# Three edits to a fused attention and feed-forward kernel: the last stores inside the Else of an If that is never taken, an interleave behind a normalisation, and two transposes a step ahead

## The chip, the cores and the metric

One core of a Trainium2 chip. The metric is the time of one execution in microseconds (us), median of several runs. Single runs scatter by about 1.2 us, as much as the effects that are looked for. So most of the argument is read from traces, and the times are used as a check. Engines in the profile: PE is TensorE (matmuls), PEld its weight loads, DVE is VectorE, ACT is ScalarE, POOL is GpSimd, SP is SyncE. A trailing q (SPq, DVEq, PEldq) marks work of an engine's instruction queue itself: branches, semaphore waits, issues of transfers.

## The reference

Causal attention with a decay bias from `s`, followed by a feed-forward layer with exact GELU. Eight batches of 576 tokens and eight heads of 64 give 4608 rows of 512.

```python
def _attn_ref(q, k, v, s):                      # q, k, v: 8 x 8 x 576 x 64, s: 8 x 8 x 576
    scores = scale * np.matmul(q, k.transpose(0, 1, 3, 2))
    cum = np.cumsum(np.maximum(s, 0.0), axis=-1)
    bias = -(cum[:, :, :, None] - cum[:, :, None, :])
    scores = np.where(causal, -1e9, scores + np.minimum(bias, 0.0))
    # ... softmax over the last axis ...
    return np.matmul(attn, v)

def _moe_ref(x, w_in, w_out):                   # 4608 x 512, 512 x 2048, 2048 x 512
    h = x @ w_in
    g = 0.5 * h * (1.0 + erf(h * inv_sqrt2))
    return g @ w_out
```

## The kernel before

The kernel works in nine chunks of 512 rows. While PE runs the feed-forward layers of chunk c (`l1_item`, `l2_item`), the attention of batch c + 1 is woven in (`sc_item`: scores and exp; `av_item`: weighted values and normalisation). The queries and keys of a later batch are interleaved by VectorE (GpSimd for batch 2), written to DRAM as rows and read back by a transposing DMA. For batches 0 and 1 PE does the transposes itself (`tr_items`); there the tile `early_q` holds the q and k of pairs 0 and 1, `early_k` those of pairs 2 and 3.

This is the weaving of chunks 1 and later, with the place of the k interleave:

```python
            late = c < 3
            for p in range(1, NP):
                # ... cut: early q interleave and transposes where not late ...
                sc_item(nb, p)
                av_item(nb, p - 1)
                l2_item(c, p, 0, 12)
                if p == NP - 1:
                    # ... cut: transposes of the rows, loads ...
                    av_item(nb, p)
                    norm_rest(nb)
                    gelu_set()
                l2_item(c, p, 12)
                # ...
                if nb + 1 < B and p == 2 and late:
                    interleave(nb + 1, "q")
                    write_rows(nb + 1, 0, nc.sync)
                if nb + 1 < B and p == 1 + late:          # late: behind q, ahead of pair 3
                    interleave(nb + 1, "k")
                    write_rows(nb + 1, 1, nc.sync)
```

The end of the program. `l2_last` does the last 128 rows in two halves of the columns; all fast pools are closed; then a flag is loaded that says whether the input leaves the range for which the fast path is right. If so, a long general path recomputes everything. With this input it is never entered.

```python
            for sub in range(4):
                if c == NCH - 1 and sub == 3:
                    l2_last(c, sub)          # two halves: 32 matmuls, copy, store each
                    break
                l2_item(c, sub, av=sub % 2 == 0)
                # ... cut: parts of the range check ...
    fast.close()

    rv = nc.values_load(bad[0:1, 0:1], min_val=0, max_val=1)
    with tc.If(rv > 0):
        # ... the general path: about 120 lines, not executed ...
```

The prologue, before the first chunk:

```python
    tr_items(0, 1, (0,))
    weights_pe()
    tr_items(0, 1, (1,))
    # ...
    sc_item(0, 1, neg=True, units=(1,))
    sc_item(0, 2, neg=True, units=(0,))
    tr_items(0, 3, (0,))
    tr_items(0, 3, (1,))
    sc_item(0, 2, neg=True, units=(1,))
```

## Time and profile before

| | before |
|---|---|
| median of the runs known ahead of the prediction | 328.77 us (327.85 to 329.01) |
| span of the profiled execution | 328.2 us |
| PE busy | 315.0 us (96%) |
| from the end of the last matmul to the end of the span | 6.01 us |

The profiled execution is one run among others, and here it was a slow one: that run took 330.29 us by the clock that gives the medians. A time is about 2 us longer than the span of its trace.

Two views of the kernel before that the prediction uses but does not show. The first is the page's line of the chain that ended last, followed back from the last instruction, as shares of the span by engine.

```profile
PE 76%; DMA 15%; POOL 4%; ACT 2%; DVE 1%; issue 1%; DVEq 0%; POOLq 0%
```

PE's matmuls make the chain for three quarters. Of the 47.6 us of DMA (15%), 37.2 are at the start, between 10.21 and 50.68, where the loads of weights and of batch 1 set the pace; the other 10.4 are the load of batch 3's k rows, 81.11 to 91.51. The second is the timeline of the last microseconds: start, duration, engine, line and operation, and in brackets the idle time before it.

```profile
318.52 3.66 PE L565 MATMUL o_ps<-w_out_r,gT 128*64 128x256 bf16 x64
...
320.47 0.42 DVE L570 COPY o_sb<-o_ps 128x256 f32<-128x256 f32 x1 [1.05 <-PE o_ps L565]
320.93 2.08 SPq L571 DMA_DIRECT2D out_dram<-o_sb  x2
322.22 0.42 DVE L570 COPY o_sb<-o_ps 128x256 f32<-128x256 f32 x1 [1.32 <-PE o_ps L565]
```

The last matmul ends at 322.19, the last copy at 322.64, the last store is issued at 322.67. Everything from there to 328.19 is landing, branch and closing waits.

### The profile page before, as it was taken

To read this page: it belongs to the slowest core of one execution; us is meant where nothing else is said; L and a number is where in the kernel's file an instruction comes from. 1 tells how busy PE (TensorE), PEld (TensorE's weight loads), DVE (VectorE), ACT (ScalarE), POOL (GpSimd) and SP (SyncE) were. 2 spreads that over 40 slices of the span, in tenths; PEclk is the share of its full clock that TensorE was granted. 3 is DMA by queue.
4 is the path that set the end of the run, shared out by engine and by line. 5 is a ranking of instruction groups with operands and counts; after the bars stand their busy time and mean duration, and the time that the engine had idled before them with its cause. 6 is when DMAs were issued, how large, how long until landed. Compare 5 with 4: busy or idle time off the path is not lost.

```text
span 328.2 us, 8740 instructions
## 1 busy us (share of the span) xinstructions
PE 315.0 (96%) x3753; PEld 182.9 (56%) x3755; DVE 191.8 (58%) x376; ACT 204.9 (62%) x292; POOL 69.6 (21%) x104
## 2 busy tenths in 40 slices
PE   7899997999999999999999999999999999999992
PEld 3566555666645556546655665556555655455562
DVE  6777446995579256937494748655884672150021
ACT  4796747759566767677667767677759676105400
POOL 8754243503400361005301700130000000000000
PEclk9999999999999999999999999999999999999998
DMA  7999999945994499967999899587700100010012
GB/s 119 222 210 208 233 188 266 245 96 43 245 281 107 88 225 241 209 97 213 257 151 158 219 272 112 106 245 193 126 2 34 65 35 2 34 64 34 1 66 72
DMA packets 53837, 47.45 MB, mean 145 GB/s; under 512 B 31328, under 2 KB 43872, under 8 KB 53792
## 3 DMA queue, kind: packets, MB, share of 16 engines
q0 software_dynamic: 15936, 23.07, 38.2%
q1 hardware_dynamic: 37856, 23.75, 30.9%
q8 instruction: 31, 0.51, 0.6%
q14 instruction: 14, 0.11, 0.1%
HBM read 36.85 MB, written 16.52 MB: 163 GB/s over the span
## 4 chain that ended last, share of the span: by engine, by line
PE 76%; DMA 15%; POOL 4%; ACT 2%; DVE 1%; issue 1%; DVEq 0%; POOLq 0%
PE h_ps L522 34%; PE o_ps L544 30%; DMA early_k<-in_k_dram 7%; DMA w_out_r<-in_moe_w_out_dram 5%; PE sc_ps L387 4%; PE avd L425 3%; PE avn L425 3%; DMA w_in_r<-in_moe_w_in_dram 3%; PE o_ps L565 1%; POOL raw_v L204 1%; PE avr L425 1%; ACT P L403 1%; POOL early_q L117 1%; POOL early_k L117 1%; POOL early_q L105 0%
## 5 line engine op out<-in xcount | busy, mean ns | idle before, releaser
L544 PE MATMUL o_ps<-w_out_r,gT 128*64 128x512 bf16 x1120 | 129.3, 380 | 0.0
L522 PE MATMUL h_ps<-xT,w_in_r 128*64 128x512 bf16 x1152 | 126.2, 379 | 0.6 <-DVE xT L461 0.6
L522 PEld LDWEIGHTS <-w_in_r 128*64 128x64 bf16 x1152 | 68.5, 110 | 56.3 <-issue 1.1
L544 PEld LDWEIGHTS <-gT 128*64 128x64 bf16 x1120 | 61.0, 110 | 49.9
L529 ACT ACTIVATE gT<-h_ps 128x1024 bf16<-128x1024 f32 x54 | 54.3, 1023 | 53.2 <-PE h_ps L522 53.2
L403 ACT ACTIVATE P<-sc_ps 128x1024 bf16<-128x1024 f32 x64 | 62.0, 1021 | 26.6 <-PE sc_ps L387 24.7
L551 DVE COPY o_sb<-o_ps 128x512 f32<-128x512 f32 x33 | 22.7, 687 | 49.1 <-PE o_ps L544 49.1
L412 DVE TENSOR_TENSOR P<-P,tri_bf 128x512 bf16<-128x512 bf16 x58 | 24.6, 432 | 42.9 <-ACT P L403 42.5
L215 DVE TENSOR_REDUCE amx<-qkT 128x2 f32<-128x1152 bf16 x32 | 40.9, 1335 | 0.0
L204 POOL DMA_DIRECT2D raw_v<-in_v_dram x40 | 34.5, 887 | 9.7 <-DMA early_q<-in_q_dram 2.5
L461 DVE SCALAR_TENSOR_TENSOR xT<-avn,ln 128x256 bf16<-128x256 f32 (+3 forms) x66 | 22.4, 386 | 20.5 <-ACT ln L442 14.0
L232 DVE TENSOR_TENSOR vv<-raw_v,wb 128x512 bf16<-128x512 f32 (+3 forms) x44 | 25.2, 632 | 0.7 <-DMA raw_v<-in_v_dram 0.7
L222 DVE TENSOR_REDUCE amv<-raw_v 128x1 f32<-128x2048 f32 (+1 forms) x16 | 23.0, 1470 | 2.3 <-DMA raw_v<-in_v_dram 2.3
L442 ACT ACTIVATE ln<-ln 128x512 f32<-128x512 f32 (+1 forms) x40 | 23.5, 587 | 1.3
L532 ACT ACTIVATE gT<-h_ps 128x512 bf16<-128x512 f32 x36 | 19.6, 602 | 6.3 <-PE h_ps L522 6.3
L441 ACT ACTIVATE ln<-avd 128x256 f32<-128x256 f32 x58 | 19.2, 391 | 6.8 <-PE avd L425 6.7
L387 PE MATMUL sc_ps<-qkT 64*128 64x256 bf16 (+2 forms) x320 | 21.1, 250 | 1.6 <-DVE qkT L372 0.6
L387 PEld LDWEIGHTS <-qkT 64*128 64x128 bf16 x320 | 12.9, 94 | 15.7 <-issue 12.4
L425 PEld LDWEIGHTS <-wb 128*64 128x64 bf16 x384 | 17.1, 110 | 4.6 <-issue 1.1
L425 PEld LDWEIGHTS <-vv 128*64 128x64 bf16 x384 | 17.6, 110 | 2.8 <-issue 1.0
L425 PE MATMUL avd<-P,wb 128*64 128x256 bf16 x232 | 16.7, 263 | 0.2 <-DVE P L412 0.2
L425 PE MATMUL avn<-P,vv 128*64 128x256 bf16 x232 | 16.0, 260 | 0.6 <-DVE xT L461 0.5
(101 smaller groups left out, 156.2 us busy)
## 6 DMA issues: line engine op xcount, KB each, us to landing
out_dram<-o_sb SPq DMA_DIRECT2D x35, 256.0 KB, 3.3
raw_v<-in_v_dram POOLq DMA_DIRECT2D x32, 256.0 KB, 8.8
rows<-qk_bf SPq DMA_DIRECT2D x12, 576.0 KB, 7.4
early_q<-in_q_dram POOLq DMA_DIRECT2D x13, 288.0 KB, 12.6
early_k<-in_k_dram POOLq DMA_DIRECT2D x13, 288.0 KB, 13.0
w_in_r<-in_moe_w_in_dram POOLq DMA_DIRECT2D x4, 512.0 KB, 11.1
w_out_r<-in_moe_w_out_dram POOLq DMA_DIRECT2D x4, 512.0 KB, 15.3
raw_v<-in_v_dram POOLq DMA_DIRECT2D x8, 128.0 KB, 11.4
```

What stands on the lines that cost most here:

```text
L204: nc.gpsimd.dma_start(out=t[:n_st, st, :, :], in_=bass.AP(tensor=v.tensor, offset=v.offset + b * H * S * D + st * 128 * D, ap=[[D, n_st], ...
L215: nc.vector.tensor_reduce(amx[:, b * NP + p], qkT[b % 2][:, :, p, :S], axis=AX, op=ALU.max, apply_absolute_value=True)
L222: nc.vector.tensor_reduce(amv[:n_st, b, j : j + 1], t[:n_st, st0:st1].rearrange("p s h d -> p (s h d)"), axis=AX, op=ALU.max, apply_absolu ...
L232: eng.tensor_tensor(vb[:n_st, st0:st1, h0:h1, :], t[:n_st, st0:st1, h0:h1, :], wb[:n_st, st0:st1, b * H + h0 : b * H + h1] .unsqueeze(3).t ...
L387: nc.tensor.matmul(s_ps[:, e, off : off + n], lhsT=qkT[b % 2][e * 64 : e * 64 + 64, 1, p, jt * 128 : jt * 128 + 128], rhs=qkT[b % 2][e * 6 ...
L403: nc.scalar.activation(P[:, :, UO[u] : UO[u] + UW[u]], s_ps[:, :, : UW[u]], func=AF.Exp, scale=scale)
L412: eng.tensor_tensor(d, d, tri_bf.unsqueeze(1).unsqueeze(1).to_broadcast([128, 2, 2, 128]), op=MULT)
L425: nc.tensor.matmul(out[e * 64 : e * 64 + 64, lo : lo + n], lhsT=(wb[:, jt, b * H + h : b * H + h + 1].to_broadcast([128, 64]) if den else ...
L442: nc.scalar.activation(ln[:, :w], ln[:, :w], func=AF.Exp, scale=-1.0)
L522: nc.tensor.matmul(h_of[c, f2][i][e * 64 : e * 64 + 64], lhsT=w_in_r[:, ko, ft * 128 + e * 64 : ft * 128 + e * 64 + 64], rhs=xT[:, ko, c * ...
L529: nc.scalar.activation(gT_of[c][:, f2 * 2 : f2 * 2 + 2, :], hh_of[c, f2], func=AF.Gelu)
L544: nc.tensor.matmul(o_ps[e * 64 : e * 64 + 64], lhsT=gT[:, ft, t0 : t0 + 64], rhs=w_out_r[:, ft, :], start=(ft == 0), stop=(ft == FT - 1), ...
```

## The change

Its intent: (1) let SyncE and VectorE take the branch while PE still works, by putting the last copies and stores into the Else; the accumulators then have to live in a new PSUM pool that is still open there; (2) let the third normalisation of chunks 1 and 2 go ahead of the k interleave on VectorE; (3) issue two PE transposes of the prologue one step earlier.

```diff
+    gT_all = const.tile([128, FT, NB], bf16, name="gT")
 ...
-            gT_of[c] = work.tile([128, FT, NB], bf16, tag="gT", bufs=1, name="gT")
+            gT_of[c] = gT_all
 ...
-    def l2_last(c, sub):
-        # ... 17 lines: two halves of the columns, matmuls, copy and store of each ...
 ...
     tr_items(0, 1, (0,))
+    tr_items(0, 1, (1,))
     weights_pe()
-    tr_items(0, 1, (1,))
 ...
+    tr_items(0, 3, (0,))
     sc_item(0, 2, neg=True, units=(0,))
-    tr_items(0, 3, (0,))
     tr_items(0, 3, (1,))
 ...
                 av_item(nb, p - 1)
+                if nb + 1 < B and p == NP - 1 and late:
+                    interleave(nb + 1, "k")
+                    write_rows(nb + 1, 1, nc.sync)
                 l2_item(c, p, 0, 12)
 ...
-                if nb + 1 < B and p == 1 + late:
+                if nb + 1 < B and p == 1 and not late:
 ...
-                if c == NCH - 1 and sub == 3:
-                    l2_last(c, sub)
+                if c == NCH - 1 and sub == 2:
                     break
 ...
     fast.close()
 
+    last = ctx.enter_context(tc.tile_pool(name="last", bufs=1))
+    lps = ctx.enter_context(tc.tile_pool(name="lps", bufs=1, space=bass.MemoryType.PSUM))
+    M = KO * 128
+    pieces = [(2, 0, M), (3, 0, M // 2), (3, M // 2, M)]
+    o_last = []
+    with tc.manual_schedule():
+        for i, (sub, m0, m1) in enumerate(pieces):
+            o_ps = lps.tile([128, M], fp32, name=f"lo_ps{i}")
+            o_last.append(o_ps)
+            # ... the 32 matmuls of the piece ...
 
     rv = nc.values_load(bad[0:1, 0:1], min_val=0, max_val=1)
-    with tc.If(rv > 0):
+    with tc.If(rv > 0) as cond:
         # ... the general path, with fewer PSUM buffers and gT_all as its g ...
+    with cond.Else():
+        for i, (sub, m0, m1) in enumerate(pieces):
+            o_sb = last.tile([128, M], fp32, name=f"lo_sb{i}")
+            r0 = (NCH - 1) * NB + sub * 128
+            nc.vector.tensor_copy(o_sb[:, : m1 - m0], o_last[i][:, : m1 - m0])
+            nc.sync.dma_start(out=out[r0 : r0 + 128, m0:m1], in_=o_sb[:, : m1 - m0])
```

More of the change, by code (lines that the diff above doesn't have):

```diff
@@ L553, in l2_item @@
         nc.sync.dma_start(out=out[r0 : r0 + 128, :], in_=o_sb)
-    def l2_last(c, sub):
-        gT = gT_of[c]
-        o_sb = work.tile([128, KO * 128], fp32, tag="osb", bufs=3, name="o_sb")
-        r0 = c * NB + sub * 128
-        for j, (tag, bufs) in enumerate((("av", 3), ("mlp", 1))):
-            m0, m1 = j * KO * 64, (j + 1) * KO * 64
-            o_ps = ps.tile([128, KO * 64], fp32, tag=tag, bufs=bufs, name="o_ps")
-            for ft in range(FT):
-                for e in range(2):
-                    t0 = sub * 128 + e * 64
-                    nc.tensor.matmul(
-                        o_ps[e * 64 : e * 64 + 64], lhsT=gT[:, ft, t0 : t0 + 64],
-                        rhs=w_out_r[:, ft, m0:m1],
-                        start=(ft == 0), stop=(ft == FT - 1), skip_group_check=True,
-                    )
-            nc.vector.tensor_copy(o_sb[:, m0:m1], o_ps)
-            nc.sync.dma_start(out=out[r0 : r0 + 128, m0:m1], in_=o_sb[:, m0:m1])
     def exp_set():
@@ L770 @@
     fast.close()
+    last = ctx.enter_context(tc.tile_pool(name="last", bufs=1))
[7 more added lines that the diff above has]
+            o_last.append(o_ps)
+            for ft in range(FT):
+                for e in range(2):
+                    t0 = sub * 128 + e * 64
+                    nc.tensor.matmul(
+                        o_ps[e * 64 : e * 64 + 64, : m1 - m0], lhsT=gT_all[:, ft, t0 : t0 + 64],
+                        rhs=w_out_r[:, ft, m0:m1],
+                        start=(ft == 0), stop=(ft == FT - 1), skip_group_check=True,
+                    )
     rv = nc.values_load(bad[0:1, 0:1], min_val=0, max_val=1)
-    with tc.If(rv > 0):
+    with tc.If(rv > 0) as cond:
         with tc.tile_pool(name="gen", bufs=1) as gen, tc.tile_pool(
@@ L812 @@
                     for n in ("q", "k"):
-                        t_ps = gps.tile([64, 1024], fp32, tag="g2", bufs=2, name="gt_ps")
+                        t_ps = gps.tile([64, 1024], fp32, tag="g2", bufs=1, name="gt_ps")
                         for st in range(ST):
@@ L826 @@
                         w = min(S, (it + 1) * 128)
-                        s_ps = gps.tile([128, 1024], fp32, tag="g2", bufs=2, name="gs_ps")
+                        s_ps = gps.tile([128, 1024], fp32, tag="g2", bufs=1, name="gs_ps")
                         for j0 in range(0, w, 512):
@@ L854 @@
                             n_j = 128 if jt < ST - 1 else SL
-                            p_ps = gps.tile([128, 128], fp32, tag="g1", bufs=2, name="gp_ps")
+                            p_ps = gps.tile([128, 128], fp32, tag="g1", bufs=1, name="gp_ps")
                             nc.tensor.transpose(
@@ L870 @@
             with tc.For_i(0, NCH, 1) as c:
-                g = gen.tile([128, FT, NB], bf16, name="gg")
+                g = gT_all
                 for ft in range(FT):
```

## The prediction

Passages of the recorded text that no trace or run of this case shows are cut, and the cuts are marked. No term of its sum is cut: it came to 327.57 us, called 327.5. Rival 3's 327.6 to 328 is an estimate, for a branch of PE that lasts longer than the 3.70 us of the trace. Where the text speaks of a queue that is full from 112 to 140 us, the trace of before has DMA at 90% or more in each slice of 0.7 us from 114.8 to 135.8. Where rival 4 says that loads are paced by landings, GpSimd stood 25.6 us at `pace` until a landing of transposed rows and then issued loads from 112.15 on. The bank numbers are those of the program as built; no trace has them, and that the bank makes PE wait is the author's assumption, which run 5 tests.

> **What bounds the kernel now**
>
> I read the page first, for which engine fills the span.
>
> ```profile
> PE 315.0 (96%) x3753; PEld 182.9 (56%) x3755; DVE 191.8 (58%) x376; ACT 204.9 (62%) x292; POOL 69.6 (21%) x104
> ```
>
> TensorE (PE) is busy for 315.0 of 328.2 us, and the change removes no matmul. So all it can win lies in 13.2 us: PE's own waits, and the two ends of the program. The waits of PE, over the whole run, are short enough to list.
>
> ```profile
> PE warm L594 <- DVE busy L127: 1.2, 1, 1.2
> PE tr_ps L366 <- DMA early_k<-in_k_dram: 1.0, 1, 1.0
> PE avw L425 <- ACT P L403: 0.9, 2, 0.5
> PE sc_ps L387 <- DVE qkT L372: 0.6, 1, 0.6
> ...
> PE avn L425 <- DVE xT L461: 0.5, 1, 0.5
> ...
> PE avd L425 <- DVE P L412: 0.2, 1, 0.2
> ```
>
> Asked by window, the last two are the only waits after 62 us; the reader is to see that the long middle has one fault. Then the timeline at that fault (about 92 us, chunk 1):
>
> ```profile
> 91.70 0.83 DVE L180 COPY qk_bf<-early_k 128x1152 bf16<-128x1152 bf16 x2 [1.52 <-DMA early_k<-in_k_dram]
> 92.44 0.75 DVE L412 TENSOR_TENSOR P<-P,tri_bf 128x512 bf16<-128x512 bf16 x2
> ...
> 93.01 0.60 PE L425 MATMUL avd<-P,wb 128*64 128x256 bf16 x8 [0.15 <-DVE P L412]
> ...
> 94.11 0.57 PE L425 MATMUL avn<-P,vv 128*64 128x256 bf16 x8 [0.51 <-DVE xT L461]
> ```
>
> VectorE stands 1.52 us for the k rows of batch 3, and the masks and the third normalisation, queued behind the interleave in order, reach PE late. Next the line of the branch, with the landing of the last store, for the end of the program:
>
> ```profile
> L774 SPq EVENT_SEMAPHORE  x8: 17/17/17, 325.9 to 326.5; - x8
> ...
> L774 PEldq COMPARE_BRANCH  x1: 3699/3699/3699, 321.4 to 321.4; - x1
> L774 DVEq COMPARE_BRANCH  x1: 72/72/72, 322.9 to 322.9; - x1
> L774 SPq COMPARE_BRANCH  x1: 58/58/58, 323.1 to 323.1; - x1
> ...
> L774 DVEq EVENT_SEMAPHORE  x1: 21/21/21, 326.1 to 326.1; - x1
> ```
> ```profile
> DMA to landing us min/median/max: 2.2/2.2/2.2
> ```
>
> After the last store (issued at 322.67, landed 2.16 later, about 324.83) SyncE branches at 323.05 and does nothing until 325.95; VectorE branches at 322.85 and resumes at 326.05; PE takes until 325.1. The landing is over before SyncE wakes: the branch, not the store, sets the end. From there SyncE works through 20 semaphore waits at 0.06 to 0.08 us each, then the closing barrier, to 328.19.
>
> [...]the three engines with long bodies in the general path lose 2.9 (SyncE), 3.1 (VectorE) and 3.7 us (PE); GpSimd, with none, goes on within 0.2 us. [...]SyncE's and VectorE's own records are 58 and 72 ns, so the rest is not the compare. [...]In the trace the q rows of batch 4 (issued 125.30) land at 136.5 and the k rows behind them (126.06) at 139.6, 13.5 us after issue[...].[...]
>
> **The change part by part**
>
> *Last stores in the Else.* The same matmuls, copies and stores stay (one copy of 0.69 us, two of 0.42, three stores), but SyncE and VectorE now branch before them. VectorE's last copy outside starts at 315.27; load of the flag 0.54 and branch bring it to about 315.9, plus 3.2 us: ready at 319.1, when the first of the three pieces (matmul end 318.68) needs it. It runs to about 319.8, ahead of the next piece at 320.4: hidden. SyncE branches at 316.4 and is ready at 319.3: hidden. PE still branches after its matmuls and arrives at its drain at PE's end (322.19) + 3.14; SyncE should arrive at its own at about +4.0 (the first four terms below, and the 1.33 us that its drain at 327.37 came after that wait), so PE stays just hidden. GpSimd and ScalarE have nothing there.
>
> New tail from PE's end: copy 0.45, issue 0.03, landing 2.16. The last store's semaphore is the second in SyncE's row (that wait came at 326.05 before), and what followed it to the end took 328.19 − 326.05 = 2.14. With 0.05 for the wake-up, the sum is 4.83 us, against 328.19 − 322.19 = 6.00 before: gain 1.15 us. Landings of these two stores were 1.7 and 2.2, so up to 1.6.
>
> *A new pool for the last accumulators.* The old kernel as built gives the `mlp` accumulator bank 0, `av` banks 1 to 3, `sc` 4 to 7; chunk 8 puts sub 0 in bank 1, sub 1 in bank 0, sub 2 in bank 3. The new pool opens when the old one is closed and should start at bank 0: that is sub 1's. Its copy runs from 315.27 for 0.69, while PE wants to start sub 2 at 315.23. PE then stalls 315.96 − 315.23 = 0.73, with the wake-up 0.75 us. I give this 75%: expected loss 0.55.
>
> *k interleave behind the third normalisation.* Chunk 1 without the fault should run as chunk 2 does: from the scores of pair 3 to the next layer takes 129.56 − 123.73 = 5.83 us there and 95.51 − 88.64 = 6.87 in chunk 1. So PE wins 1.04 us. The copies (2 x 0.45) would run after the normalisation, about 93.1, with the data there since 91.5; the next normalisation comes at 94.5, so they fit. In chunk 2 PE has no fault to remove: gain 0.
>
> But PE being early meets a transfer. The scores of batch 4 need its first k transpose:
>
> ```profile
> L196 SPq DMA_TRANSPOSE qkT<-rows x1: 1128/1128/1128, 139.6 to 139.6; - x1
> ...
> DMA to landing us min/median/max: 4.1/4.1/4.1
> ```
> ```profile
> 144.33 0.78 PE L387 MATMUL sc_ps<-qkT 64*128 64x256 bf16 x10
> ```
>
> It lands at 139.60 + 4.08 = 143.68, only 0.65 before its use at 144.33. The k rows that feed it wait in a full queue, so writing them 1.9 us later (128.0[...]) should not move them; but nothing moves them earlier either. PE can win 0.6 there and waits for the other 0.4. **0.6 us.**
>
> *Prologue transposes a step ahead.* VectorE idles 1.22 us before the copies of pair 3 and PE 0.62 for them; a transpose a step ahead may bring the first layer 0.2 to 0.6 us forward. At 50.72 PE waits 0.97 us for early_k of batch 1, and the chain of waits leads back from there through transfers alone (w_out at 21.56, early_k at 38.02 to 50.68) to w_in at 10.21. That landing does not depend on PE, so the wait grows by what was won. **0.0.**
>
> *The rest* (gT in the constant pool, fewer buffers in the general path, not executed): 0.[...]
>
> Sum: 328.77 − 1.15 + 0.55 − 0.6 − 0.0 = 327.57; I call it **327.5 us**.
>
> **The rivals**
>
> 1. No bank stall: the new pool takes a bank that is free. For it: only one of three pieces conflicts.[...] Then 326.9.
> 2. The k rows land later, because the write now queues behind more loads: transposes, and then the scores of batch 4 (144.33), slip. For it: 0.65 us of slack and the queue full from 112 to 140 us. Against: [...]q rows ahead. A slip of 1.3 us eats the whole 0.6 and more: 328.5 to 329.
> 3. PE's branch becomes the last at the barrier: it is only 0.9 us ahead of SyncE in the sum above[...]. Then 327.6 to 328.
> 4. The transfers come forward with PE and all parts add: 1.04 + 1.15 + 0.4 = 2.6, 326.2. Against: the loads are paced by their own landings.
>
> **Range and chances**
>
> Three runs of before spread over 1.2 us (327.85 to 329.01), as large as the gain. The rivals span 326.2 to 329, the outer ones unlikely. Range **326.4 to 328.5**. Two per cent is 6.6 us, half of all that PE does not fill, and no part reaches that: faster 0.01, same 0.98, slower 0.01.
>
> **What would show it**
>
> The tail: SyncE's and VectorE's branches near 316, the last store's issue to the end about 4.3 us instead of 5.5. The bank: a PE wait of about 0.75 us on the copy of sub 1, the first matmul of sub 2. The middle: no PE wait near 93 us, and a new one of about 0.4 us on a transpose at the scores of batch 4. The prologue: the wait for early_k at 50.7 grown from 1.0 us while its end stays. It is wrong if the scores of batch 4 start after 144.3, if the end stays 6 us after PE's last matmul, or if early_k's landing moves with the prologue.

## The result, and the profile after

| | before | after |
|---|---|---|
| median | 328.89 us (327.85 to 329.16, 4 runs) | 326.59 us (326.09 to 326.7, 4 runs) |
| ratio of fast runs, 95% interval | | 0.9933 (0.9909 to 0.9957) |
| span of the profiled execution | 328.2 us | 324.7 us |
| from the end of the last matmul to the end of the span | 6.01 us | 4.07 us |

A ratio here is the mean time of one kernel's fast runs over that of the other's of the same rounds, so it is not quite the ratio of the medians. The result is 2.3 us by the medians, within the predicted range; by the 2% mark it counts as the same.

The page of the changed kernel, busy times and chain:

```profile
PE 316.0 (97%) x3755; PEld 183.9 (57%) x3755; DVE 191.1 (59%) x376; ACT 205.0 (63%) x292; POOL 69.8 (21%) x104
...
PE 81%; DMA 11%; POOL 4%; ACT 2%; issue 1%; DVE 0%; POOLq 0%; DVEq 0%
```

No engine's work has changed. PE's busy time is 1.0 us above that of before; this trace holds two more matmul records, and the ends of matmuls are modelled, so I read nothing into it. The chain holds less of DMA, 36.2 us against 47.6: the 10.4 us of batch 3's k rows are not in it. In this execution PE waits for loads only 0.3 us, at the start. The waits of PE, first over the whole run (the waiting line, whom it waits for, us in total, times, longest):

```profile
PE warm L577 <- DVE busy L128: 1.2, 1, 1.2
PE lo_ps L769 <- DVE o_sb L552: 0.8, 1, 0.8
...
PE tr_ps L367 <- DMA early_q<-in_k_dram: 0.3, 1, 0.3
```

Asked for the time after 62 us alone, the second of these is the only one left. The reader is to see three things against the list of before: the two waits near 93 us are gone; a new one has come, the first matmul of the new accumulators on VectorE's copy of sub 1; and the wait for `early_k`, 1.0 us before, is not in the list at all. (Lines are one to two numbers apart between the kernels, because of the added lines.)

Chunk 1, the same stretch as the one that the prediction shows of before:

```profile
90.70 0.82 DVE L462 SCALAR_TENSOR_TENSOR xT<-avn,ln 128x256 bf16<-128x256 f32 x3 [0.65 <-ACT ln L443]
91.13 0.55 PE L426 MATMUL avd<-P,wb 128*64 128x256 bf16 x8
91.43 0.82 DVE L181 COPY qk_bf<-early_k 128x1152 bf16<-128x1152 bf16 x2
91.57 0.57 PE L426 MATMUL avn<-P,vv 128*64 128x256 bf16 x8
```

VectorE now runs the normalisation first and then the copies, and it no longer idles before them; PE's two groups have no idle time in brackets.

The end of the program in the timeline:

```profile
312.73 0.69 DVE L552 COPY o_sb<-o_ps 128x512 f32<-128x512 f32 x1 [2.76 <-PE o_ps L545]
...
313.47 7.14 PE L769 MATMUL lo_ps<-w_out_r,gT 128*64 128x512 bf16 x96 [0.79 <-DVE o_sb L552]
317.31 0.69 DVE L897 COPY lo_sb<-lo_ps 128x512 f32<-128x512 f32 x1 [3.89 <-PE lo_ps L769]
318.02 3.41 SPq L898 DMA_DIRECT2D out_dram<-lo_sb  x3
...
320.65 0.42 DVE L897 COPY lo_sb<-lo_ps 128x256 f32<-128x256 f32 x1 [1.32 <-PE lo_ps L769]
```

And the branch's own line, with the number of records, their durations in ns and the times of the first and the last:

```profile
L776 DVEq COMPARE_BRANCH  x1: 72/72/72, 313.4 to 313.4; - x1
L776 SPq COMPARE_BRANCH  x1: 58/58/58, 313.8 to 313.8; - x1
L776 PEldq COMPARE_BRANCH  x1: 3662/3662/3662, 319.9 to 319.9; - x1
```

VectorE branches at 313.36 and goes on at 316.63, 0.7 us ahead of its first copy in the Else; SyncE branches at 313.83 and goes on at 316.90. Both branches lie under PE's matmuls, but for 0.1 us of VectorE's, which falls into PE's wait. PE's own branch still stands behind its matmuls and lasts to 323.55, 2.94 us after the end of the last one (320.61).

The last lines are SyncE's waits around the landing of the last store. In before the landing (324.83) came while SyncE stood in its branch; its 20 waits, 8 of them shown in the prediction and 12 here, all followed. In after 7 of them are left from the landing on:

```profile
L916 SPq EVENT_SEMAPHORE  x12: 28/28/28, 326.6 to 327.2; - x12
...
DMA to landing us min/median/max: 2.2/2.2/2.2
...
L924 SPq EVENT_SEMAPHORE  x7: 28/28/120, 323.3 to 323.7; - x7
```

The first line is of before, the others are of after: the landing of the last store (issued at 321.10), and the waits behind it. The wait of 120 ns is the one for PE's semaphore: SyncE stands there from 323.57 to 323.69, and PE, out of its branch at 323.55, has its own semaphore record from 323.61 to 323.66.

### Where the 3.5 us between the two traces are

I cut each trace at points that all kernels have: the start of the first matmul of the first layer in chunks 0, 2 and 3, the start of the last one of chunk 1's first layer ("end" in the tables), the end of the last matmul of all, and the end of the span. Times in us:

| stage | before | after | difference |
|---|---|---|---|
| start to the end of chunk 1's first layer | 73.47 | 71.90 | -1.57 |
| from there to chunk 2's first layer | 22.04 | 21.07 | -0.97 |
| chunk 2's first layer to chunk 3's | 34.05 | 34.05 | 0.00 |
| from there to the last matmul's end | 192.62 | 193.59 | +0.97 |
| last matmul's end to the end of the span | 6.01 | 4.07 | -1.94 |

The sum is -3.51. The last four rows are stretches in which edits (1) and (2) act. The first row could be the prologue, chance, or something else in the change; a load has part in it. The last bytes of batch 1's k rows landed at 50.68 in the trace of before, where PE waited 0.97 us for them, and at 49.70 in that of after, where it did not. What the experiments below have to settle: is the first row part of the change's gain; is the new wait a matter of the bank, as predicted; and why is the tail's gain 1.9 instead of the predicted 1.15.

### The profile page after: what moved, and what is told of

It reads as the page before. It is cut to its first block, busy times and chain, and to the rows that moved or that the text cites. A ratio compares the mean times of both kernels' runs of the same rounds, so it can differ in the third digit from the quotient of the medians.

```text
span 324.7 us, 8755 instructions
## 1 busy us (share of the span) xinstructions
PE 316.0 (97%) x3755; PEld 183.9 (57%) x3755; DVE 191.1 (59%) x376; ACT 205.0 (63%) x292; POOL 69.8 (21%) x104
## 4 chain that ended last, share of the span: by engine, by line
PE 81%; DMA 11%; POOL 4%; ACT 2%; issue 1%; DVE 0%; POOLq 0%; DVEq 0%
PE h_ps L523 34%; PE o_ps L545 33%; DMA w_out_r<-in_moe_w_out_dram 5%; PE sc_ps L388 4%; PE avd L426 4%; DMA early_k<-in_k_dram 4%; PE avn L426 3%; DMA w_in_r<-in_moe_w_in_dram 3%; PE lo_ps L769 2%; PE avr L426 1%; POOL raw_v L205 1%; ACT P L404 1%; POOL early_q L117 1%; POOL early_k L117 1%; POOL w_out_r L250 0%
## 5 line engine op out<-in xcount | busy, mean ns | idle before, releaser
L545 PE MATMUL o_ps<-w_out_r,gT 128*64 128x512 bf16 x1088 | 125.9, 380 | 0.0
L545 PEld LDWEIGHTS <-gT 128*64 128x64 bf16 x1088 | 59.2, 110 | 48.3
L552 DVE COPY o_sb<-o_ps 128x512 f32<-128x512 f32 x32 | 22.0, 687 | 46.3 <-PE o_ps L545 46.3
```

The costliest lines, as they stand in the source:

```text
L545: nc.tensor.matmul(o_ps[e * 64 : e * 64 + 64], lhsT=gT[:, ft, t0 : t0 + 64], rhs=w_out_r[:, ft, :], start=(ft == 0), stop=(ft == FT - 1), ...
```

## The experiments

Theories. **Mine:** the tail gains about 1.9, the k interleave about 1.0 where the stall occurs, the new pool loses about 1.0, the prologue gains nothing, and the first row is scatter of a transfer. **Rivals:** the first row is a gain of the prologue order; the loss at the pool is a conflict of one bank; the k interleave in its new place pays for its gain later, at the scores of batch 4. (A further rival, that the first row belongs to edit (1), was not tested; the point-by-point account below comes back to it.)

Twelve kernels were run, all with right results, each timed in five rounds against the kernel before of the same rounds. The stage table of all traces stands behind the last run.

### Run 1, before_again: the kernel before, unchanged

```diff
(no change)
```

> The kernel before, unchanged, as a control. Theory A (all of the gain is of the edits): ratio 1.000 within 0.002, and the k rows of batch 1 that PE waits for at about 50 us land at 50.7 again, with PE waiting about 1.0 us. Theory B (part of the 3.5 us between the two profiles is the transfers' own scatter): ratio still 1.000, but that landing lies elsewhere, 49.5 to 50.7, and PE's first matmul of chunk 0's second layer stage, of chunk 1 and so on move with it by up to 1.5 us.

328.88 us (327.49 to 331.55) against 328.49 (327.5 to 332.19); ratio 0.999 (0.9948 to 1.0033). So five rounds leave about 0.4% open, or 1.4 us. The profiled run was the slowest one, with its first loads late and the start of the first layer at 22.17 instead of 20.09. It has no wait of PE after 62 us at all, and its chunk 1 took 21.06 instead of 22.04. The stall that edit (2) removes is thus itself not in every execution of the kernel before: it is there when PE is early against the k rows of batch 3 (figures of seven traces stand behind the last table).

### Run 2, tail_only: edit (1) alone

```diff
+    gT_all = const.tile([128, FT, NB], bf16, name="gT")
-    def l2_last(c, sub): ...
+    # pools last and lps, three pieces, copies and stores in cond.Else(), as in the change
```

> Only the stores in the Else, with the new accumulator pool; interleave and prologue as before. From the profile after: PE's last matmul to the end 4.0 us instead of 6.0, less the 0.79 us that PE waits before the first of the new pieces: gain 1.2 us, ratio 0.9964 (0.995 to 0.998). My prediction's sum for this part was 0.6 us, ratio 0.998. Rival: the branch was hidden anyway and the gain is of the other parts: ratio 1.000.

327.22 us (326.48 to 328.09), ratio 0.9951 (0.9908 to 0.9993). Its trace has both waits after 62 us:

```profile
PE lo_ps L766 <- DVE o_sb L552: 0.8, 1, 0.8
PE avn L426 <- DVE xT L462: 0.5, 1, 0.5
```

The tail is 4.10 and the last stretch of PE 193.60: the gain at the end and the loss at the pool both belong to edit (1), and the stall of chunk 1 (here 21.66) stays without edit (2). This trace also has the earliest end of chunk 1's first layer but one (71.86), with the old order of the prologue: its k rows of batch 1 landed at 48.31. That speaks against the prologue as the cause of the first row.

### Run 3, k_only: edit (2) alone

```diff
                 av_item(nb, p - 1)
+                if nb + 1 < B and p == NP - 1 and late:
+                    interleave(nb + 1, "k")
+                    write_rows(nb + 1, 1, nc.sync)
...
-                if nb + 1 < B and p == 1 + late:
+                if nb + 1 < B and p == 1 and not late:
```

> Only the interleave of k behind the third normalisation. Theory A (the transfers come forward with PE): PE loses its 0.66 us of waits at about 93 us, stays 1.0 us ahead to the end: ratio 0.997. Theory P (as predicted: the first k transpose of batch 4 holds PE up): a new PE wait of about 0.4 us at the scores of batch 4, 0.6 us kept: ratio 0.998. Both: no PE wait between 90 and 95 us.

328.12 us (326.9 to 328.8), ratio 0.9971 (0.993 to 1.0013). No wait of PE after 62 us. Chunk 1 is 21.07, and what comes after takes 34.05 and 192.62 as in before, so nothing is paid back later. The first transpose of batch 4's k rows landed at 142.50 and was used at 143.16: it came 1.2 us earlier than in before (143.68), as PE did, and had a lead of 0.67, as in before (0.65). In this trace the transfer came forward with PE and did not hold it up.

### Run 4, prologue_only: edit (3) alone

```diff
     tr_items(0, 1, (0,))
+    tr_items(0, 1, (1,))
     weights_pe()
-    tr_items(0, 1, (1,))
...
+    tr_items(0, 3, (0,))
     sc_item(0, 2, neg=True, units=(0,))
-    tr_items(0, 3, (0,))
```

> Only the prologue's order. Theory P (as predicted: swallowed by the wait for the k rows of batch 1 at about 50 us): first layer starts 0.2 to 0.6 us earlier, ratio 1.000 (0.999 to 1.001). Rival: that wait has slack in most runs, and the gain comes through: ratio 0.998 to 0.9985, with no PE wait on that landing.

328.75 us (328.55 to 330.26), ratio 0.9994 (0.9954 to 1.0034): nothing. The first layer starts at 19.85 instead of 20.09, but chunk 1's first layer ends at 74.61, later than in before, as the k rows of batch 1 landed at 51.56. PE's waits between 21 and 62 us:

```profile
PE tr_ps L366 <- DMA early_k<-in_k_dram: 1.3, 1, 1.3
PE avn L425 <- DVE vv L232: 0.9, 1, 0.9
```

The first has grown from 1.0 to 1.3. But the lead of 0.24 did not get as far as that wait. The second, which before does not have, comes earlier (about 48 us): VectorE scales the values of batch 1 late, as it was itself held by a load for 1.5 us. PE then stood at the transposes at 50.29, 0.54 later than in before (49.75), and waited longer there because the landing was 0.88 later.

### Run 5, after_bank: the changed kernel with its three accumulators in other banks

```diff
+    banks = [lps.tile([128, M], fp32, name=f"lo_ps{i}") for i in range(3)]
     with tc.manual_schedule():
         for i, (sub, m0, m1) in enumerate(pieces):
-            o_ps = lps.tile([128, M], fp32, name=f"lo_ps{i}")
+            o_ps = banks[(i + 1) % 3]
```

> The changed kernel with the three last accumulators rotated over their banks, so that the first of them takes the bank of sub 0 of the last chunk, long evacuated, instead of the bank of sub 1. Theory as predicted (the wait is for the bank): PE's wait of 0.79 us before the first piece is gone, 0.75 us faster than the changed kernel, ratio about 0.991 to before. Rival (the wait is for the whole closed pool, so for its last copy, whatever the bank): the wait of 0.79 us stays, ratio as the changed kernel, 0.993.

326.64 us (326.06 to 327.48) against 329.2 (327.96 to 331.52); ratio 0.992 (0.9881 to 0.9959). The wait is where it was:

```profile
PE lo_ps L770 <- DVE o_sb L552: 0.8, 1, 0.8
```

If the predicted reason were right, the first piece would now start in a bank that is free, and the wait would be gone or move to another piece. It isn't: the first matmul in the new pool waits for the last copy out of the closed pool in both orders of the banks, and sub 1 has only one bank. In time this kernel is a twin of the changed one.

### Run 6, after_kept_bank: one accumulator in a pool that stays open

```diff
+    mps = ctx.enter_context(tc.tile_pool(name="mps", bufs=1, space=bass.MemoryType.PSUM))  # ahead of fast
     # all tiles of tag "mlp" (warm, avn of the last pair, o_ps) from mps instead of ps
...
-                l2_item(c, sub, av=sub % 2 == 0)
+                l2_item(c, sub, av=sub % 2 == 0 or c == NCH - 1)
...
-            o_ps = lps.tile([128, M], fp32, name=f"lo_ps{i}")
+            o_ps = lps.tile(...) if i else mps.tile([128, M], fp32, tag="mlp", bufs=1, name="lo_ps0")
```

> The changed kernel, but the bank of the first of the last three pieces belongs to a pool that stays open across the end of the fast path; sub 1 uses one of the other accumulators. If the wait is for the closed pool, it is gone here: PE runs from sub 1 into sub 2 without the 0.79 us, the end stays 4.0 us after PE's last matmul: 0.7 to 0.8 us faster than the changed kernel, ratio about 0.991 to before. Rival: VectorE, which needs until about 3.9 us after sub 1's end to be through the branch, is then late for the first piece and the end is 4.4 us after PE's last matmul: 0.4 us faster only.

326.2 us (324.99 to 326.78), ratio 0.9905 (0.9865 to 0.9945). The end in its timeline:

```profile
308.62 3.62 PE L546 MATMUL o_ps<-w_out_r,gT 128*64 128x512 bf16 x32
...
312.07 7.11 PE L770 MATMUL lo_ps<-w_out_r,gT 128*64 128x512 bf16 x96
312.28 0.69 DVE L553 COPY o_sb<-o_ps 128x512 f32<-128x512 f32 x1 [2.76 <-PE o_ps L546]
```

PE starts the last pieces before the copy of sub 1 has begun, and no wait is left after 62 us. This run changes two things, as sub 1 also goes to another accumulator; but run 5 had shown that a free bank alone does not help, so it is the pool. VectorE is late for the first piece here, as the rival in the expectation says (its copy starts at 316.34), but in time for the last one, and the tail does not grow. PE's last stretch is back at 192.62, the tail 4.14. It also shows why a wait of 0.79 cost 0.97: in an unbroken stream the next group starts 0.17 before the modelled end of the one before it (308.62 + 3.62 = 312.24, next start 312.07); a wait loses this overlap too. Of all kernels run this has the shortest trace (323.33) and, with run 7, the lowest times; it is faster than the kernel before. By times alone it is not told apart from the changed kernel or from its neighbour of the same rounds, the twin of run 5 (326.2 against 326.64, ranges overlapping); the 0.97 is read from the traces.

### Run 7, no_branch: the kernel before without the flag and the general path

```diff
-    rv = nc.values_load(bad[0:1, 0:1], min_val=0, max_val=1)
-    with tc.If(rv > 0):
-        # ... the general path ...
```

This gives a kernel that is right for this input only: it measures what the branch costs in all.

> The kernel before without the general path and its branch (right on these inputs, not a kernel to keep). If the far branch is what the end of the kernel before pays for: from PE's last matmul to the end 3.9 to 4.1 us instead of 6.0, no PE stall, ratio 0.994. If the end were set by the landing and the closing semaphores alone: 5.5 us or more, ratio 0.998 to 1.000.

326.22 us (324.73 to 326.64), ratio 0.9898 (0.9857 to 0.9939). The tail is 3.52, shorter than the expected 3.9 to 4.1, so the branch cost 6.01 - 3.52 = 2.5 us in before, and the Else saves 1.9 of these. Its last store:

```profile
DMA to landing us min/median/max: 1.7/1.7/1.7
```

Here SyncE sat at the wait for the last store until 323.37, and 1.28 us followed. So without any branch the end is set by the landing, and by seven waits and the closing barrier behind it. Of the 0.55 us by which the changed kernel's tail is longer, 0.4 is a slower landing of the last store (2.2 us) and 0.1 the rest behind it. Most of this 0.1 is SyncE's wait for PE, whose branch ends at 323.55: that wait lasts 105 to 138 ns in all six traces with the new end, and the waits around it 28.

The DMA queue that the profile names "instruction" (q14) moves near the branches. In before two packets of 8 KB of it start at 324.17, 1.1 and 1.3 us after SyncE and VectorE branch; in after such packets start at 314.42 and 315.11, again 1.1 and 1.3 us after the branches. In the trace of run 7 this queue has no packet after 270 us. The times fit engines that wait at the branch for these packets; no run shows that they do.

### Run 8, k_and_prologue: edits (2) and (3)

```diff
(the diffs of runs 3 and 4 together)
```

> The two parts in the middle and at the start, without the tail. If they add up with the tail (1.2 us) to the changed kernel's 2.2 us: 1.0 us faster than before, ratio 0.997. If the prologue contributes what lies between: 0.9955.

328.61 us (327.18 to 328.79), ratio 0.9967 (0.9926 to 1.0007), so no more than run 3. Chunk 1 21.06, tail 5.90, PE's last stretch 192.62; the first k transpose of batch 4 is 0.96 ahead of its use. No wait of PE follows from the early start.

### Run 9, late_transposes: before, with the two transposes that need the late load moved behind other work

```diff
             l2_item(c, 3, 0, 4)
-            tr_items(1, 2, (0, 1), ..., wide=True)
-            tr_items(1, 3, (0, 1), ..., wide=True)
             scale_pair(1, 2)
             av_item(1, 1, rest=False)
-            scale_pair(1, 3)
             l2_item(c, 3, 4, 8)
-            sc_item(1, 2)
+            tr_items(1, 2, (0, 1), ..., wide=True)
+            tr_items(1, 3, (0, 1), ..., wide=True)
+            scale_pair(1, 3)
             l2_item(c, 3, 8, 12)
+            sc_item(1, 2)
             sc_item(1, 3)
```

> The kernel before, with PE's transposes of pairs 2 and 3 of batch 1, which wait for the k rows landing at 48 to 52 us, moved behind av of pair 1 and four more f tiles of the second layer, some 1.7 us of PE work. If that landing is what PE's place at the end of the first layer of chunk 1 follows, PE's wait there is gone or under 0.3 us in the trace, and the kernel is 0 to 1 us faster than before (ratio 0.997 to 1.000; the scores of pair 2 may wait for the copies, up to 0.8 us, and give part back). If PE is held elsewhere: ratio 1.000 and the same time from the first layer of chunk 0 to that of chunk 1.

329.6 us (329.32 to 330.71) against 328.45 (327.62 to 329.42); ratio 1.0051 (1.003 to 1.0072), the slowest of all. The wait for the load is gone, but so is any gain: the scores now stand behind what they need (PE's waits between 21 and 62 us):

```profile
PE sc_ps L387 <- ACT P L403: 1.0, 2, 0.5
PE avw L425 <- ACT P L403: 0.5, 1, 0.5
PE sc_ps L387 <- DVE qkT L372: 0.5, 2, 0.3
```

As an improvement it is a miss. As an instrument it serves: a kernel in which PE waits for no load between 21 and 62 us.

### Run 10, late_transposes_prologue: run 9 with edit (3)

```diff
(the diffs of runs 9 and 4 together)
```

> The same and the prologue's new order. If the prologue's gain was swallowed by that landing (as predicted), it comes through here: the first layer of chunk 0 starts about 0.4 us earlier and that of chunk 1 ends 0.4 us earlier than in the run beside it, ratio 0.001 lower. If the new order gains nothing anywhere: equal starts. The landings scatter by over a microsecond, so the trace's stages are to tell, not the ratio.

329.09 us (328.86 to 329.34), ratio 1.0024 (1.0006 to 1.0041). Against run 9, of the same rounds, the start of the first layer is 0.44 earlier (20.02 against 20.46), the end of chunk 1's first layer 0.25 earlier (73.38 against 73.63), and the median 0.5 lower. In this one pair of traces, then, the new order of the prologue brings PE forward by some tenths, and with no wait for a load part of it arrives; in runs 4 and 8 none was seen to arrive in the times.

### Run 11, kept_bank_late_transposes: runs 6 and 9 together

```diff
(the diffs of runs 6 and 9 together, on the changed kernel)
```

> The changed kernel with the accumulator bank kept open (0.98 us of PE at the end) and the transposes moved: if both hold, below both kernels and below the kept bank alone: 325.5 us where that had 326.2, ratio 0.988 to 0.9905. If the moved transposes only shift the wait: as the kept bank alone, 0.9905.

327.37 us (326.49 to 328.38), ratio 0.9965 (0.9946 to 0.9984). A miss: worse than the kept bank alone, 1.2 us by the medians, though from other rounds. Chunk 0 has, next to the waits of run 9, another:

```profile
PE avd L427 <- DVE P L414: 1.6, 2, 0.9
```

Its load had landed early (48.56). In run 6 it did too (48.49), and PE did not wait for it, so there was probably nothing for the moved transposes to win. Why VectorE was late with `P` is not shown.

### Run 12, after_again: the changed kernel, unchanged

```diff
(no change)
```

> The changed kernel, unchanged, as a second control, for its own scatter. If the gain is the tail (1.9), less the wait on the closed pool (1.0), and the repaired chunk 1 (up to 1.0): 1.9 us, ratio 0.994; the first result's 0.9933 and the 0.992 of the kernel with rotated banks would be the same within scatter. In the trace: chunk 1 from the end of its first layer to chunk 2's 21.07 us, 193.6 us from the first layer of chunk 3 to PE's end, tail 4.1 us, each within 0.1; the start up to the end of chunk 1's first layer anywhere from 71.5 to 74.5 us.

327.45 us (325.94 to 330.06) against 328.28 (327.17 to 329.59); ratio 0.9973 (0.9935 to 1.0011). One of its six runs took 330.06. The stages are those of the changed kernel, but the end of chunk 1's first layer is at 72.92 and not 71.90, with the load at 50.00. So the changed kernel's gain is smaller here than in the first measurement, 0.8 us by the medians.

### All traces

Columns: landing of batch 1's k rows; start of the first layer; end of chunk 1's first layer; from there to chunk 2's first layer; from chunk 3's first layer to the last matmul's end; last matmul's end to the end of the span; span. The stretch between chunk 2's and chunk 3's first layers is 34.05 in every one.

| kernel | load landed | start | chunk 1 layer ends | chunk 1 | chunk 3 on | tail | span |
|---|---|---|---|---|---|---|---|
| before | 50.68 | 20.09 | 73.47 | 22.04 | 192.62 | 6.01 | 328.19 |
| before_again | 49.63 | 22.17 | 75.72 | 21.06 | 192.62 | 6.00 | 329.45 |
| prologue_only | 51.56 | 19.85 | 74.61 | 21.07 | 192.62 | 5.89 | 328.25 |
| k_only | 50.36 | 20.09 | 73.28 | 21.07 | 192.62 | 5.77 | 326.79 |
| k_and_prologue | 50.50 | 19.79 | 73.04 | 21.06 | 192.62 | 5.90 | 326.67 |
| late_transposes | 50.89 | 20.46 | 73.63 | 21.07 | 192.62 | 5.85 | 327.22 |
| late_transposes_prologue | 50.68 | 20.02 | 73.38 | 21.06 | 192.62 | 5.85 | 326.96 |
| no_branch | 49.99 | 20.62 | 73.05 | 21.42 | 192.61 | 3.52 | 324.65 |
| tail_only | 48.31 | 20.20 | 71.86 | 21.66 | 193.60 | 4.10 | 325.26 |
| after | 49.70 | 20.31 | 71.90 | 21.07 | 193.59 | 4.07 | 324.68 |
| after_again | 50.00 | 19.92 | 72.92 | 21.06 | 193.59 | 3.86 | 325.49 |
| after_bank | 50.02 | 19.58 | 72.64 | 21.07 | 193.59 | 4.10 | 325.45 |
| after_kept_bank | 48.49 | 19.59 | 71.45 | 21.07 | 192.62 | 4.14 | 323.33 |
| kept_bank_late_transposes | 48.56 | 20.16 | 74.43 | 21.07 | 192.62 | 4.12 | 326.29 |

The tail is 5.77 to 6.01 in the seven traces with the old end and the branch (mean 5.90), and 3.86 to 4.14 in the six with the new one (mean 4.07).

Seven kernels have the k interleave at its old place. In four of them chunk 1 takes 21.06 or 21.07; the k rows of batch 3 landed there 11.2 to 17.0 us after the end of chunk 1's first layer. In the other three they landed 17.42 (no_branch), 17.65 (tail_only) and 18.04 us (before) after it, and chunk 1 took 21.42, 21.66 and 22.04: each tenth by which the rows are later costs a tenth. So the stall is worth 0.28 us in the mean of these seven traces.

## Why the prediction was right or wrong, point by point

**The tail: right in kind, too small.** The stated steps held in the main: both branches were taken under PE's matmuls and VectorE was ready before its first copy. PE's branch, called just hidden, was hidden but for about 0.1 us. But the gain is 1.9 (1.8 by the means over all traces) and not 1.15; by the prediction's own figures it should have read 6.00 - 4.83 = 1.17. Of the sum of five terms, four hold: copy, issue and wake-up came to 0.50 against 0.53, the landing to 2.16, as carried over. The step that failed is "what followed it to the end took 328.19 − 326.05 = 2.14". In the changed kernel 1.41 us followed the wait for the last store (323.27 to 324.68). The prediction carried over a queue of waits that had all become due at once while SyncE stood in the branch. In the Else SyncE does most of them while the last store is still in flight: by 322.13 it had passed ten, and only the wait for that store itself and six more were left. Run 7 shows the same remainder, 1.28. This is 0.73 of the missing 0.76.

**The new pool: the loss was there, its reason was wrong, its size a little low.** The step "the new pool ... should start at bank 0: that is sub 1's" failed as a cause: other banks leave the wait as it is (run 5), a pool that is never closed removes it (run 6). The loss is in all four traces that have the new pool as built or with its banks rotated (0.97 or 0.98), where the prediction gave it 75%, and it was 0.97 and not 0.75, since a wait also loses the 0.17 by which matmul groups overlap. So the expected 0.55 was 0.42 too low.

**The k interleave: the gain right, the deduction wrong.** 1.04 was predicted for chunk 1; 0.97 was measured against the trace of before. The step "nothing moves them earlier either" failed: the first k transpose of batch 4 landed 1.2 us earlier in run 3 and 3.0 us earlier in the changed kernel (140.70 against 143.68), and in no trace did PE wait for it. So the deduction of 0.4 was not due; the gain is the full 0.97. But the baseline was not what the prediction took it for: the stall is in one of the two traces of the kernel before and not in the other (run 1), nor in run 4. The mean gain of this edit lies between 0 and 0.97 (0.28 by the seven traces with the old place), and run 3 puts it at 0.3% with an interval that includes zero.

**The prologue: the number right, the step in part.** Nothing in total (run 4). PE starts 0.2 to 0.5 earlier in most traces with the new order, and loads take the lead, as said. But it was not always the wait for `early_k`: in runs 4 and 8 the lead was lost before it, wholly or in part, in a wait for VectorE's scaled values (0.9 and 0.2 us); in runs 5 and 12 PE came to the transposes 0.5 and 0.3 us earlier than in before and did wait there (0.8 and 0.6). Without a wait for a load part of the lead came through (runs 9 and 10, one pair). One condition is missing from the step: it holds while PE is at the transposes before the load. Where the load landed early (48.31 in run 2, 48.49 in run 6), PE did not wait for it, and chunk 1's first layer ended at 71.86 with the old order and at 71.45 with the new one: one pair of traces, and so no more than a hint of 0.4 us.

**The profiles' first row: not predicted, and open.** The 1.57 us agree in size with two waits between 21 and 62 us that the trace of before has and that of after has not: 0.97 for `early_k` and 0.6 for VectorE's `xT`. The landing of that load ranged from 48.31 to 51.56 over 14 traces. The order of the prologue does not sort it: the mean is 49.98 in the six traces with the old order and 49.94 in the eight with the new one. Edit (1) may: the six kernels with the new end landed at 48.31 to 50.02 (mean 49.2), the seven with the old end and the branch at 49.63 to 51.56 (mean 50.6). Among the ten of these kernels that leave chunk 0's transposes in place, the five with the new end finish chunk 1's first layer at 71.45 to 72.92, the five with the old end at 73.04 to 75.72. Edit (1) also moves `gT` to another pool, and no run had that alone. With one trace of each kernel this is a hint; whether the first row is chance or comes with edit (1) is not shown, nor what sets the landing.

**The sum.** By the traces the edits are worth 1.9 at the end, less 0.97 at the pool, plus 0 to 0.97 in chunk 1: between 0.9 and 1.9 us. The prediction had 1.2. The measured differences of the medians were 2.3 (first measurement), 0.8 (run 12) and, for the twin of run 5, 2.6; if the first row should belong to edit (1), its worth is larger than this sum. With the terms as the traces of this pair have them, the prediction's own sum would have been 327.57 - 0.79 (tail) - 0.37 (interleave) + 0.42 (pool) = 326.83, against 326.59 measured. So the range held the result though three of the terms were off by 0.4 to 0.8 us each, of which one had the other sign: that they partly cancelled is luck, and so is part of the agreement, as the first row is in the measured traces and not in the sum. The remaining 0.24 us is well within the scatter. Rival 1 (no stall) and rival 2 (later k rows) are refuted; rival 3 has begun: SyncE's own drain (323.86) comes 0.1 us later because SyncE waits for PE's semaphore at 323.66, so a much larger gain at the end would need PE's branch to go as well. Rival 4 was right about batch 4's transfers: the first k transpose came forward with PE (landed at 142.50 in run 3 against 143.68).

## What to carry to other kernels

If a program ends with a branch over a long block, put the last copies and stores behind the branch in the block that is taken, so that every engine but the busiest takes the branch under the matmuls. Here the branch held SyncE for 2.9 us in before and 3.1 in after, VectorE for 3.2 and 3.3, and PE for 3.70 and 3.66 (one record), while the records of the compare itself are 45 to 72 ns on the other four engines. In after the first two lay beside PE's matmuls, but for 0.1 us of VectorE's. Then count the waits that are left behind the last landing, and don't carry over a queue of waits that were all due at once: in before these were 20 on SyncE, 0.06 to 0.10 us apart and 1.36 us in all, where the prediction read 0.06 to 0.08. Accumulators for that block should come from a pool that was open all along, since here the first matmul in a pool opened behind a closed one waited for the last copy out of the closed one (0.79 us of wait, 0.97 of PE's time, with either order of banks; no wait with a pool that stayed open). Whether this is of the chip or only of how the program's waits were placed, no run shows. Before a saving of half a microsecond is credited to an edit, look whether the kernel before shows the stall in a second trace, and whether a load lies between the edit and the end: the same load landed between 48.31 and 51.56 us over 14 traces, 10.8 to 12.8 us after its issue.
